# One batch of attention ahead of the products instead of two, in a fused attention and cosine feed-forward kernel

## The chip, the core and the metric

The kernel runs on one core of a Trainium2 chip. The metric is the time of one execution in microseconds on the device. Engines are called as in the profile: PE (TensorE), DVE (VectorE), ACT (ScalarE), POOL (GpSimd), and SP, whose queue issues most DMAs.

## The reference

```
# q, k, v: 8 batches, 8 heads, 576 positions, 64 dims
scores = (q @ k^T) / 8
heads 0-3 see keys with 0 <= i - j < 32; heads 4-7 keys with i >= j and i % 32 == j % 32
attn = softmax(masked scores);  o = attn @ v
x = o as 4608 tokens x 512
h = x @ w_in          # w_in 512 x 2048, double precision
g = h * cos(h)
out = g @ w_out       # w_out 2048 x 512, double precision
```

## The kernel before

**Attention by units.** A batch has 10 units: four "strided" ones (two pairs of heads, two halves of the residues) and six "local" ones (three stretches of 192 positions, two pairs of heads). A unit is a Python generator with three stages: scores and softmax; transposes of the probabilities; products with v. `schedule` lays these stages over numbered steps, `step(steps, n)` emits those of step n. KNOTS says how many units are begun by which step.

Units come in two kinds. With `plain` the softmax uses ACT's Exp, and the mask is written into the score bank by a matmul (L173). The others use two Silu passes and a square, since Silu and Sin share ACT's table, and add the mask on DVE. A unit loads q and k (`qk`) and v on SP's queue.

The results go to a DRAM tensor `xT`, 512 rows by 4608 tokens, by DMAs on ACT's queue (L260 and L320).

**The products by blocks and chunks.** A block is 384 tokens (12 blocks). A chunk is one of 16 pieces of 128 of the 2048 hidden columns, so there are 192 chunks. Both operands of each product are split into a rounded part and a rest (`hi`, `lo`), and three of the four products are taken. `hidden` (L345 and on) makes h with 12 matmuls of 384 columns, then g by ACT and DVE, then g's two parts; `outer` (L367) adds g times w_out into three accumulators, 9 matmuls of 512 columns. `outer` runs LAG = 3 chunks behind `hidden`. h has two banks.

`load_x(j)` brings block j's four pieces from `xT` into `x_raw`, casts them on DVE (L335) and subtracts on POOL (L336).

**The weights.** They arrive as doubles. `load_weight` (L111 to L130) loads 128 x 512 of them (512 KB) into one of two buffers `raw`, makes float32 words of them with three DVE passes (L116, L119, L125) and one ACT pass (L124), casts on ACT (L129) and subtracts on POOL (L130). Chunk f needs one such piece of w_in and one of w_out: 32 loads in all. From chunk AHEAD on, the conversion for chunk f is ordered behind the DVE reduction (L349) of chunk f - AHEAD of block 0.

**The order.** First the 20 plain units of batches 0 and 1, with `load_x(0)` and `load_x(1)` among them and some matmuls that only keep PE busy (L417). Then blocks 0 and 1 side by side: chunk f of block 0, then chunk f - 1 of block 1, so that each weight serves two chunks as it comes in. Then three chunks of block 2. Then one loop over the other chunks, with the 60 units of batches 2 to 7 among them.

The kernel is written in program order, but a scheduler fills each engine's queue: an instruction whose inputs and buffers are there may go ahead of earlier ones that wait. So a queue's order isn't the program's.

Of the kernel before, what the change touches and what calls it, by code (L numbers as in the profile page):

```python
# [36 lines left out]
NSU = -(-NG // SU)  # L37
MASKED = -8.0e9             # times the scale: the reference's -1e9
# [5 lines left out]
TB = 384                    # tokens of a block  # L44
# [8 lines left out]
LOADS = (12, 20)  # L53
# [15 lines left out]
def attention_cos_ffn(ctx, tc, qkl, vl, qkvs, w_in, w_out, eye, eye16, mask_l0, mask_l, mask_s, out):  # L69
# [7 lines left out]
    xp = ctx.enter_context(tc.tile_pool(name="xp", bufs=2))  # L77
# [10 lines left out]
    shift1, shift2 = (const.tile([P, 1], F32, name=n) for n in ("shift1", "shift2"))  # L88
    for t, value in ((shift1, -SHIFT), (shift2, -SHIFT - STEP)):
# [21 lines left out]
    def load_weight(cv, src, hi, lo, after):  # L111
        """src: 128 x 512 doubles; hi + lo: their float32."""
# [9 lines left out]
        # A double's upper word as a float32 has the exponent's upper eight bits; scaled, its exponent and mantissa  # L122
        # are the float32's, three bits too far right. What is below a float32's range becomes nothing.
# [279 lines left out]
    with ExitStack() as loading:  # L403
        cv = loading.enter_context(tc.tile_pool(name="cv", bufs=2))
        with ExitStack() as stack:
# [19 lines left out]
            for n in range(max(steps) + 1):  # L425
# [3 lines left out]
                if n == LOADS[0]:  # L429
                    x0 = load_x(0)  # L430
# [135 lines left out]
```

## Time and profile before

| | |
|---|---|
| three runs | 1002.9, 1004.25, 1005.04 us |
| median | 1004.25 us |
| span of the profiled execution, first to last instruction | 1000.8 us |
| median of the runs less that span | 3.45 us |
| PE busy | 984.5 us (98%) |
| ACT busy | 572.9 us (57%) |
| DVE busy | 464.6 us (46%) |
| POOL busy | 381.9 us (38%) |

The profiled execution has no time of its own beside its span; what lies around the span is taken as the 3.45 us. "Busy" is the union of an engine's instructions, and matmuls overlap one another, so the mean time of one matmul is longer than the time it adds; distances between starts tell what it adds. Rows of busy time by stretch read: stretch, its length, busy time of each engine with its number of instructions, granted clock of PE as a share of full speed, share of the DMA engines, GB/s. Rows of one line alone have only the engines that run that line.

### The profile page before, as it was taken

The page shows a single profiled execution, that of the slowest core. Times are in us where ns is not written, and L with a number is a line of the kernel's source. Part 1 is how long each engine was busy: PE and PEld are TensorE (multiplying, and loading weights), DVE is VectorE, ACT ScalarE, POOL GpSimd, SP SyncE. Part 2 cuts the span into 40 slices and gives each one's busy share as a digit, 9 for nine tenths or more (in the row PEclk, how much of TensorE's full clock was granted, in tenths as well). Part 3 has the DMA queues.
Part 4 walks back from the last instruction along what each step waited for, and adds up shares of the span by engine and source line. Part 5 has one row for each costly group of instructions (what it writes and reads, how often), then busy time and mean ns, then how long its engine had stood idle before and what let it go on. Part 6 is the DMA issues. An engine that isn't in the chain of part 4 may idle for free.

```text
span 1000.8 us, 17954 instructions
## 1 busy us (share of the span) xinstructions
PE 984.5 (98%) x6890; PEld 841.0 (84%) x6890; DVE 464.6 (46%) x1004; ACT 572.9 (57%) x1235; POOL 381.9 (38%) x418
## 2 busy tenths in 40 slices
PE   9989999999999999999999999999999999999998
PEld 5768877888888888888888888888888888889997
DVE  6866777645544444444344344434443444322222
ACT  3666666666665555555555555555655555544543
POOL 2654544624443443333333343323333333322222
PEclk9999999999999999999999999999999999999999
DMA  7963333122332223112212122211211221100000
GB/s 249 303 196 121 110 107 125 59 90 73 103 90 81 85 68 97 50 49 69 78 44 82 50 87 58 78 50 53 84 58 39 88 63 43 48 9 1 32 1 32
DMA packets 48230, 80.15 MB, mean 80 GB/s; under 512 B 5904, under 2 KB 33296, under 8 KB 48144
## 3 DMA queue, kind: packets, MB, share of 16 engines
q1 hardware_dynamic: 38208, 69.35, 22.3%
q10 hardware_dynamic: 9936, 9.65, 2.8%
q8 instruction: 54, 0.88, 0.4%
q14 instruction: 32, 0.26, 0.1%
HBM read 60.11 MB, written 18.87 MB: 79 GB/s over the span
## 4 chain that ended last, share of the span: by engine, by line
PE 84%; DMA 7%; DVE 5%; issue 2%; ACT 1%; POOL 0%; SPq 0%; ACTq 0%; DVEq 0%; POOLq 0%
PE h L345 37%; PE acc L367 35%; DMA raw<-in_w_out 4%; PE acc L238 3%; DVE raw L116 2%; PE acc L303 2%; PE acc L254 2%; PE acc L279 2%; PE acc L246 1%; DVE raw L119 1%; DVE raw L125 1%; DMA qk<-in_qkl 1%; PE acc L291 1%; PE acc L417 1%; DMA x_raw<-xT 1%
## 5 line engine op out<-in xcount | busy, mean ns | idle before, releaser
L360 POOL TENSOR_TENSOR g_lo<-r,g_hi 128x384 fp32r<-128x384 f32 x192 | 196.5, 1024 | 369.5 <-issue 246.6
L345 PE MATMUL h<-x_hi,wi_h 128*128 128x384 f32 x768 | 273.3, 356 | 7.8 <-DVE r L356 7.8
L345 PE MATMUL h<-x_lo,wi_h 128*128 128x384 f32 x768 | 259.1, 337 | 0.4 <-POOL x_lo L336 0.4
L345 PE MATMUL h<-x_hi,wi_l 128*128 128x384 f32 x768 | 259.4, 338 | 0.0
L349 DVE SCALAR_TENSOR_TENSOR r<-r,h 128x384 f32<-128x384 int32 x192 | 106.3, 554 | 276.1 <-ACT r L348 270.1
L367 PE MATMUL acc<-wo_l,g_hi 128*128 128x512 f32 x576 | 228.0, 396 | 0.0
L367 PE MATMUL acc<-wo_h,g_hi 128*128 128x512 f32 x576 | 227.7, 395 | 0.0
L367 PE MATMUL acc<-wo_h,g_lo 128*128 128x512 f32 x576 | 225.5, 396 | 0.0
L348 ACT ACTIVATE r<-h 128x384 int32<-128x384 f32 x192 | 93.9, 489 | 158.0 <-PE h L345 128.3
L345 PEld LDWEIGHTS h<-x_hi,wi_h 128*128 128x128 f32 x768 | 144.5, 188 | 27.5 <-DVE r L356 17.7
L356 DVE SCALAR_TENSOR_TENSOR r<-r,h 128x384 f32<-128x384 f32 x192 | 105.9, 552 | 107.3 <-ACT r L355 107.2
L345 PEld LDWEIGHTS h<-x_lo,wi_h 128*128 128x128 f32 x768 | 145.0, 189 | 3.0 <-POOL x_lo L336 0.7
L352 ACT ACTIVATE r<-r 128x384 f32<-128x384 f32 x192 | 100.2, 522 | 79.6 <-DVE r L349 79.5
L359 ACT CAST g_hi<-r 128x384 fp32r<-128x384 f32 x192 | 98.2, 511 | 82.8 <-DVE r L356 80.3
L345 PEld LDWEIGHTS h<-x_hi,wi_l 128*128 128x128 f32 x768 | 144.7, 188 | 0.2
L367 PEld LDWEIGHTS acc<-wo_h,g_lo 128*128 128x128 f32 x576 | 108.2, 188 | 24.9
L367 PEld LDWEIGHTS acc<-wo_h,g_hi 128*128 128x128 f32 x576 | 108.1, 188 | 18.1 <-ACT g_hi L359 0.3
L367 PEld LDWEIGHTS acc<-wo_l,g_hi 128*128 128x128 f32 x576 | 108.2, 188 | 17.9
L355 ACT ACTIVATE r<-r 128x384 f32<-128x384 f32 x192 | 100.4, 523 | 4.5
L336 POOL TENSOR_TENSOR x_lo<-x_raw,x_hi 128x384 fp32r<-128x384 f32 x48 | 50.6, 1057 | 107.7 <-DVE x_hi L335 106.8
L195 POOL TENSOR_TENSOR t_sb<-t_sb,mx 128x288 f32<-128x288 f32 (+1 forms) x60 | 41.5, 692 | 47.3 <-DVE mx L194 42.0
L214 POOL TENSOR_TENSOR e_sb<-e_sb,z 128x288 f32<-128x288 f32 x48 | 31.9, 666 | 40.0 <-DVE z L212 21.0
(66 smaller groups left out, 884.0 us busy)
## 6 DMA issues: line engine op xcount, KB each, us to landing
qk<-in_qkvs SPq DMA_DIRECT2D x32, 324.0 KB, 3.2
qk<-in_qkl SPq DMA_DIRECT2D x48, 208.0 KB, 2.5
x_raw<-xT SPq DMA_DIRECT2D x48, 192.0 KB, 2.4
out<-o SPq DMA_DIRECT2D x36, 256.0 KB, 2.1
raw<-in_w_in SPq DMA_DIRECT2D x16, 512.0 KB, 3.6
raw<-in_w_out SPq DMA_DIRECT2D x16, 512.0 KB, 3.6
v<-in_vl SPq DMA_DIRECT2D x48, 144.0 KB, 2.3
xT<-x_t ACTq DMA_DIRECT2D x16, 288.0 KB, 3.6
```

The costliest lines, as they stand in the source:

```text
L195: nc.gpsimd.tensor_tensor(out=t, in0=t, in1=mx[:, :n].unsqueeze(2).broadcast_to([P, n, w]), op=ALU.subtract)
L214: nc.gpsimd.tensor_tensor(out=pn, in0=e, in1=z[:, :n].unsqueeze(2).broadcast_to([P, n, w]), op=ALU.mult)
L336: nc.gpsimd.tensor_tensor(out=lo, in0=raw, in1=hi.bitcast(F32), op=ALU.subtract)
L345: nc.tensor.matmul(h, w[:, f, c], x[c], start=(i == 0), stop=(i == len(ops) - 1))
L348: nc.scalar.activation(out=k, in_=h, func=AF.Copy, scale=1.0 / (2.0 * math.pi))
L349: red = nc.vector.scalar_tensor_tensor(out=r, in0=k, scalar=-2.0 * math.pi, in1=h, op0=ALU.mult, op1=ALU.add)
L352: sin = nc.scalar.activation(out=r, in_=r, func=AF.Sin, scale=0.5)
L355: nc.scalar.activation(out=r, in_=r, func=AF.Square)
L356: nc.vector.scalar_tensor_tensor(out=r, in0=r, scalar=0.5, in1=h, op0=ALU.subtract, op1=ALU.mult)
L359: nc.scalar.copy(out=g_hi, in_=r)
L360: nc.gpsimd.tensor_tensor(out=g_lo, in0=r, in1=g_hi.bitcast(F32), op=ALU.subtract)
L367: nc.tensor.matmul(acc[t], g[:, ts], w[:, f], start=(f == 0 and i == 0), stop=(f == NFC - 1 and i == 2))
```

## The change

- Only the 10 units of batch 0 run as plain units ahead of the products. The 70 units of batches 1 to 7 are units of the Silu kind among the chunks.
- Blocks are no longer paired: one loop over all 192 chunks, with the weights' conversions among block 0's 16 chunks and units from its first step on. AHEAD is 3 instead of 2.
- Block 0's x doesn't go through `xT`: a unit's result is cast and subtracted straight from its SBUF tile (`keep`, `split_x`); the other columns are written as before.
- `load_x` loads into the tile of the low part instead of a buffer of its own.
- cos(h) is sin(r + pi/2) with the bias in a tile, where it was 1 - 2 sin(r/2)^2: the ACT pass for the square goes, DVE's last pass becomes a plain product, and the final copies lose their factor of -2.
- The units' tile `e_sb` has 2 buffers instead of 3, `v` 3 instead of 4, `o` 2 instead of 3 in the loop.

```
-AHEAD = 2
+AHEAD = 3
-KNOTS = ((LAG, 0), (9.5, 8), (25, 16), (121, 56), (131, 60))
-UNIT_LAG = 3
+KNOTS = ((0, 0), (9, 6), (52, 26), (100, 46), (148, 66), (164, 70))
+UNIT_LAG = 2
...
-            e = self.wk.tile([P, SU * GB], F32, name="e_sb", bufs=4 if self.plain else 3)
+            e = self.wk.tile([P, SU * GB], F32, name="e_sb", bufs=4 if self.plain else 2)
...
-            v = self.ld.tile([P, VS], F32, name="v", bufs=4)
+            v = self.ld.tile([P, VS], F32, name="v", bufs=3)
...
-            nc.scalar.dma_start(out=xT[:, 2 + p, at:at + LU * QB], in_=x_t)
+            self.keep(2 + p, b * S + u * LU * QB, x_t)
+
+        def keep(self, c, at, x_t):
+            n = x_t.shape[1]
+            first = min(max(TB - at, 0), n)
+            if first:
+                split_x(x_t[:, :first], x0[0][c][:, at:at + first], x0[1][c][:, at:at + first])
+            if first < n:
+                nc.scalar.dma_start(out=xT[:, c, at + first:at + n], in_=x_t[:, first:])
...
+    def split_x(x, hi, lo):
+        nc.vector.tensor_copy(out=hi, in_=x)
+        nc.gpsimd.tensor_tensor(out=lo, in0=x, in1=hi.bitcast(F32), op=ALU.subtract)
...
-            raw = xp.tile([P, TB], F32, name="x_raw")
+            raw = lo.bitcast(F32)
...
-        nc.scalar.activation(out=k, in_=h, func=AF.Copy, scale=1.0 / (2.0 * math.pi))
+        nc.scalar.activation(out=k, in_=h, func=AF.Copy, scale=1.0 / (2.0 * math.pi), bias=0.25)
...
-        sin = nc.scalar.activation(out=r, in_=r, func=AF.Sin, scale=0.5)
+        sin = nc.scalar.activation(out=r, in_=r, func=AF.Sin, bias=quarter)
...
-        nc.scalar.activation(out=r, in_=r, func=AF.Square)
-        nc.vector.scalar_tensor_tensor(out=r, in0=r, scalar=0.5, in1=h, op0=ALU.subtract, op1=ALU.mult)
+        nc.vector.tensor_tensor(out=r, in0=r, in1=h, op=ALU.mult)
...
+        units = att.units(0)
+        steps = schedule(units, ((0, 0), (len(units), len(units))), 2)
...
+        steps = schedule([unit for b in range(1, B) for unit in att.units(b)], KNOTS, UNIT_LAG)
+        nxt = x0
+        for n in range(NTB * NFC):
+            j, f = n // NFC, n % NFC
             if f == 0:
                 cur, acc = nxt, accumulators(ps_o)
+            if j == 0:
+                need_weights(cv, f)
             step(steps, n)
             if f == LOAD_AT and j + 1 < NTB:
                 nxt = load_x(j + 1)
             chunk(j, f, cur, acc)
+            if j == 0:
+                need_weights(cv, min(f + AHEAD, NFC - 1))
```

More of the change, by code (lines that the diff above doesn't have):

```diff
@@ L326, in units, with x_operands @@
             ]
[L328 to L333 removed]
+    def split_x(x, hi, lo):
+        nc.vector.tensor_copy(out=hi, in_=x)
+        nc.gpsimd.tensor_tensor(out=lo, in0=x, in1=hi.bitcast(F32), op=ALU.subtract)
+    def x_operands():
+        return tuple([xs.tile([P, TB], F32R, name=name) for _ in range(NKC)] for name in ("x_hi", "x_lo"))
+    def load_x(j):
+        his, los = x_operands()
+        for c, (hi, lo) in enumerate(zip(his, los)):
+            raw = lo.bitcast(F32)
             nc.sync.dma_start(out=raw, in_=xT[:, c, j * TB:(j + 1) * TB])
[L335 to L338 removed]
+            split_x(raw, hi, lo)
         return his, los
@@ L401, in step @@
             next(unit, None)
-    with ExitStack() as loading:
-        cv = loading.enter_context(tc.tile_pool(name="cv", bufs=2))
-        with ExitStack() as stack:
-            ps = stack.enter_context(tc.tile_pool(name="ps", bufs=1, space=bass.MemoryType.PSUM, reuse_waits="tile"))
-            att = Attention(
-                stack, True, ((ps_h, "h"), (ps_h, "h"), (ps, "acc0")), ((ps_o, "acc0"), (ps_o, "acc1")),
-                ((ps_o, "acc2"), (ps, "acc3")), ld_bufs=3,
-            )
-            steps = schedule(att.units(0) + att.units(1), ((0, 0), (20, 20)), 2)
-            spare = ps.tile([P, 512], F32, name="acc2")
-            def keep_busy(n, after):
-                for _ in range(n):
-                    mm = nc.tensor.matmul(
-                        spare[:64], warm, warm.unsqueeze(1).broadcast_to([P, 8, 64]), start=True, stop=True
-                    )
-                    if after is not None:
-                        order(mm, after, "in its place")
-                    after = mm
-            keep_busy(BUSY[0], None)
-            for n in range(max(steps) + 1):
-                step(steps, n)
-                if n + 1 < len(BUSY):
-                    keep_busy(BUSY[n + 1], att.scored)
-                if n == LOADS[0]:
-                    x0 = load_x(0)
-                if n == LOADS[1]:
-                    x1 = load_x(1)
-        gp = ctx.enter_context(tc.tile_pool(name="gp", bufs=LAG + 1, side="right", reuse_waits="tile"))
-        with ExitStack() as stack:
-            op = stack.enter_context(tc.tile_pool(name="op", bufs=2, reuse_waits="tile"))
-            ps_o1 = stack.enter_context(
-                tc.tile_pool(name="ps_o1", bufs=1, space=bass.MemoryType.PSUM, reuse_waits="tile")
-            )
-            acc0, acc1 = accumulators(ps_o), accumulators(ps_o1)
-            for f in range(NFC + 1):
-                if f < NFC:
-                    need_weights(cv, f)
-                    chunk(0, f, x0, acc0)
-                    need_weights(cv, min(f + AHEAD, NFC - 1))
-                if f >= 1:
-                    chunk(1, f - 1, x1, acc1)
-            cur, acc = load_x(2), accumulators(ps_o)
-            for f in range(LAG):
-                chunk(2, f, cur, acc)
@@ L454, in attention_cos_ffn, with keep_busy @@
-    with ExitStack() as stack:
-        op = stack.enter_context(tc.tile_pool(name="op", bufs=3, reuse_waits="tile"))
+    x0 = x_operands()
+    cv = ctx.enter_context(tc.tile_pool(name="cv", bufs=2))
+    with ExitStack() as stack:
+        ps = stack.enter_context(tc.tile_pool(name="ps", bufs=1, space=bass.MemoryType.PSUM, reuse_waits="tile"))
+        att = Attention(
+            stack, True, ((ps_h, "h"), (ps_h, "h"), (ps, "acc0")), ((ps_o, "acc0"), (ps_o, "acc1")),
+            ((ps_o, "acc2"), (ps, "acc3")), ld_bufs=3,
+        )
+        units = att.units(0)
+        steps = schedule(units, ((0, 0), (len(units), len(units))), 2)
+        spare = ps.tile([P, 512], F32, name="acc2")
+        def keep_busy(n, after):
+            for _ in range(n):
+                mm = nc.tensor.matmul(
+                    spare[:64], warm, warm.unsqueeze(1).broadcast_to([P, 8, 64]), start=True, stop=True
+                )
+                if after is not None:
+                    order(mm, after, "in its place")
+                after = mm
+        keep_busy(BUSY[0], None)
+        for n in range(max(steps) + 1):
+            step(steps, n)
+            if n + 1 < len(BUSY):
+                keep_busy(BUSY[n + 1], att.scored)
@@ L456, in attention_cos_ffn @@
+    gp = ctx.enter_context(tc.tile_pool(name="gp", bufs=LAG + 1, side="right", reuse_waits="tile"))
+    op = ctx.enter_context(tc.tile_pool(name="op", bufs=2, reuse_waits="tile"))
+    with ExitStack() as stack:
         ps = stack.enter_context(tc.tile_pool(name="ps", bufs=1, space=bass.MemoryType.PSUM, reuse_waits="tile"))
         att = Attention(stack, False, *(((ps, f"acc{i}"),) for i in range(3)), ld_bufs=2)
-        steps = schedule([unit for b in range(2, B) for unit in att.units(b)], KNOTS, UNIT_LAG)
```

25 lines of the change are left out of this document (6 added, 19 removed).

## The prediction

> **What bounds the kernel now.** I read the page's totals first, then the busy time by stage, then the chain that ended last, and then the rows of the weight conversion.
>
> ```profile
> span 1000.8 us, 17954 instructions
> PE 984.5 (98%) x6890; PEld 841.0 (84%) x6890; DVE 464.6 (46%) x1004; ACT 572.9 (57%) x1235; POOL 381.9 (38%) x418
> ...
> L355 ACT ACTIVATE r<-r 128x384 f32<-128x384 f32 x192 | 100.4, 523 | 4.5
> ```
> ```profile
> 0.00:48.60 48.60, 45.81 (x674) 30.75 (x675) 36.03 (x110) 24.11 (x59) 21.54 (x31) 1.00 0.86 279
> 48.60:75.00 26.40, 21.21 (x162) 17.90 (x160) 16.19 (x33) 17.68 (x40) 14.27 (x14) 0.95 0.62 194
> 98.00:187.00 89.00, 85.36 (x403) 70.91 (x402) 65.51 (x97) 60.02 (x115) 44.63 (x38) 1.00 0.34 113
> 200.00:873.00 673.00, 673.00 (x4871) 579.24 (x4870) 292.30 (x672) 389.31 (x863) 250.06 (x288) 1.00 0.23 69
> ```
> The columns are stretch, length, then busy time of PE, PEld, DVE, ACT and POOL. From 200 to 873 us PE is busy 673.00 of 673.00: there the time is the sum of PE's work, and other engines have room (ACT 389). All that can be lost or won lies before 200 us, where attention and weights come first. So I price PE's work, and then ask how long PE waits early on.
>
> ```profile
> 916.39 2.11 PE h L345 x12
> ...
> 987.91 2.11 PE h L345 x12
> 990.02 5.84 PE acc L367 x25
> ```
> ```profile
> 200.00:1000.80 800.80, 376.23 (x1920) 330.66 (x1920) 1.00 0.20 60
> ```
> ```profile
> 200.00:1000.80 800.80, 367.31 (x1462) 271.67 (x1460) 1.00 0.20 60
> ```
> The first fence is the chain: 17 chunks lie between its first two rows, (987.91 - 916.39) / 17 = 4.207 us a chunk, half of it the 12 matmuls of `hidden`, half the 9 of `outer`. The work ends at 995.86; 4.94 us of copy, store and end follow. The other two, busy time of one line's instructions, count L345 and L367 after 200 us: 1920/12 = 160 hidden halves and 1462/9 = 162.4 outer halves, 322.4 x 2.1035 = 678.2 us. Of 795.86 us, 117.7 are left for 60 units of attention: **1.95 us of PE a unit**.
>
> Now the weights. The chain runs through them between 98 and 187 us.
>
> ```profile
> 144.27 3.51 DMA raw<-in_w_out
> ...
> 153.56 3.63 DMA raw<-in_w_out
> ```
> ```profile
> L116 DVE TENSOR_SCALAR raw<-raw x32: 385/859/1547, 12.2 to 185.4; 128x512 int32<-128x512 int32 x32
> L119 DVE SCALAR_TENSOR_TENSOR raw<-raw x32: 678/694/1684, 13.4 to 186.6; 128x512 int32<-128x512 int32 x32
> L124 ACT ACTIVATE raw<-raw x32: 658/666/712, 14.1 to 187.4; 128x512 f32<-128x512 f32 x32
> L125 DVE SCALAR_TENSOR_TENSOR raw<-raw x32: 649/693/1250, 15.3 to 188.1; 128x512 int32<-128x512 int32 x32
> ...
> L129 ACT CAST wi_h<-raw x16: 656/667/680, 15.9 to 184.2; 128x512 fp32r<-128x512 f32 x16
> L130 POOL TENSOR_TENSOR wi_l<-raw,wi_h x16: 1307/1316/1787, 16.7 to 185.0; 128x512 fp32r<-128x512 f32 x16
> ...
> DMA to landing us min/median/max: 3.4/3.6/6.7
> ```
> Loads of w_out start 153.56 - 144.27 = 9.29 us apart. `raw` has two buffers, one for w_in's chunk and one for w_out's, and a buffer takes its next load only when L130 is through with it. So a buffer's own loop is the DMA, three DVE, two ACT steps and one POOL step; by medians, with L116 at its shortest, 3.6 + 0.385 + 0.694 + 0.666 + 0.693 + 0.667 + 1.316 = 8.0 us. The missing 1.3 us are mostly L116, whose median is 0.859; two rows of the timeline say why:
>
> ```profile
> 143.68 0.85 DVE L116 TENSOR_SCALAR raw<-raw 128x512 int32<-128x512 int32 x1
> ```
> ```profile
> 142.93 1.31 POOL L130 TENSOR_TENSOR wo_l<-raw,wo_h 128x512 fp32r<-128x512 f32 x1
> ```
> It starts while L130 runs on POOL and ends 0.29 us after POOL's end (144.24). Sixteen pairs at 9.29 us are 149 us, whatever PE does. Before, two chunks share each pair, 2 x 4.207 = 8.4 us of PE per 9.29, so PE hardly waits: 85.36 of 89.00.
>
> **The change, part by part.**
>
> *Ten units leave the front.* Before, chunk 0 waits for x0, which goes through HBM (rows of the timeline: start, length, engine and line):
>
> ```profile
> 36.80 0.32 ACT L258 COPY x_l<-acc 128x192 f32<-128x192 f32 x1
> ```
> ```profile
> 43.42 0.90 SPq L334 DMA_DIRECT2D x_raw<-xT  x2
> ```
> ```profile
> 48.60 0.42 PE L345 MATMUL h<-x_hi,wi_h 128*128 128x384 f32 x1
> ```
> The last copy that block 0 needs ends at 37.1, its loads are issued at 43.4, and the product starts at 48.6. On chip it is one cast and one subtraction, about 1.5 us, so 38.6 without anything else; and as batch 1's units no longer stand among batch 0's on DVE I take 32 (ends: 28 and 40). The cast waits for ACT's copy, and on DVE softmaxes and conversions stand behind it; six casts in place of eight, so I count nothing for that. The other end matters little, since the weights come later still. The writes of block 0's part of xT on ACT's queue and its four loads on SP's go. The mask matmuls of ten units go too, in time that was idle.
>
> *The same ten units come back in the loop*, as Silu units: 10 x 1.95 = 19.5 us of PE, certain. In total PE's work after the front is 192 x 4.207 + 70 x 1.95 = 944.2 us, with the tail 949.2. From 32 us on that would be 981 us if PE never waited.
>
> *Block 0 takes the weights alone.* One chunk and few units stand against each pair. First the start: with AHEAD = 3, f = 2 waits for no chunk.
>
> ```profile
> 28.91 1.32 POOL L130 TENSOR_TENSOR wi_l<-raw,wi_h 128x512 fp32r<-128x512 f32 x1 [2.26 <-ACT wi_h L129]
> ```
> ```profile
> 33.28 0.38 SPq L114 DMA_DIRECT2D raw<-in_w_in  x1
> ```
> ```profile
> 53.98 1.31 DVE L116 TENSOR_SCALAR raw<-raw 128x512 int32<-128x512 int32 x2
> ```
> Before, f = 1's buffer is free at 30.2, the load of f = 2 is issued at 33.3 (SP stood behind x's and v's loads), and its conversion starts at 53.98, after chunk 0's reduction. After, load at 30, landing at 33.6, L116 at 34: the stream is 20 us earlier. From there 13 periods lead to f = 15, and the rest of the loop, 9.29 - 3.6 = 5.7 us, to its split weights. The period's ends are 8.0 and about 10.5 (both L116 at its longest, 2 x (1.547 - 0.859) = 1.4 more); I take 9.29, the row nearest to it, as unit work replaces the second chunk's. So 34 + 13 x 9.29 + 5.7 = 160.5, and 162.6 with the last hidden half.
>
> *What PE can do meanwhile.* Sixteen hidden and 13 outer halves (61.0 us), and units. By the order of steps alone 6 + (16 - 9) x 20/43 = 9.3 units are begun at step 16. But the queues are filled ahead: weights already convert at 12.2 us here, though the program has them after all attention. So I let units run until DVE is full (two groups of the page, then busy times of three stretches, the second for the casts of x alone):
>
> ```profile
> L349 DVE SCALAR_TENSOR_TENSOR r<-r,h 128x384 f32<-128x384 int32 x192 | 106.3, 554 | 276.1 <-ACT r L348 270.1
> L356 DVE SCALAR_TENSOR_TENSOR r<-r,h 128x384 f32<-128x384 f32 x192 | 105.9, 552 | 107.3 <-ACT r L355 107.2
> ```
> ```profile
> 116.56:125.84 9.28, 8.90 (x43) 7.40 (x43) 6.92 (x11) 6.28 (x13) 4.70 (x4) 1.00 0.33 113
> ```
> ```profile
> 200.00:873.00 673.00, 13.72 (x35) 1.00 0.23 69
> ```
> ```profile
> 15.00:45.00 30.00, 28.85 (x470) 20.55 (x468) 27.96 (x85) 18.33 (x48) 17.54 (x21) 1.00 0.87 282
> ```
> A chunk costs DVE 1.106 us. A pair of weights with two chunks keeps it 6.92, with one 5.81. A unit costs at most (292.30 - 13.72 for x's casts - 132 x 1.106) / 60 = 2.2 us (132 chunks: 160 less the (990.0 - 873) / 4.207 = 28 after 873). In the front DVE reached 27.96 of 30, 93%; of 9.29 that is 8.65, so (8.65 - 5.81) / 2.2 = 1.29 units a period, 17.6 over 13.6 periods, and one at the start: 18.6 units (ends: 9.3 and 22).
>
> *Cosine as sine.* ACT loses one pass a chunk, 523 ns (L355), and its Sin takes a bias tile; DVE's last pass stays one pass over the same two operands. At 389 of 673 us ACT isn't what PE waits for, so 0; in block 0 it takes 0.5 us from ACT's 6.28 a period, where DVE is fuller. The shorter path from h to g ends a last chunk sooner, hidden behind the 5.84 us of outer halves at the end.
>
> *Fewer buffers* (e_sb 3 to 2, v 4 to 3, o 3 to 2), load_x into x_lo, the knots: between 0 and some 5 us if a unit came late in the loop; 0 taken, as PE was never idle there, and the units (after block 0 some 51 to 176 chunks) come no closer than before (60 to 157). Should one be late, its transposes wait on PE's queue and the chunk's matmuls stand behind them.
>
> **Sum.** 162.6 + 176 x 2.1035 + 179 x 2.1035 + (70 - 18.6) x 1.95 + 4.94 = 162.6 + 746.7 + 100.2 + 4.9 = 1014.4 us of span. The three runs have a median of 1004.25, 3.45 over the profiled span, so **1017.9, say 1017 us, 1.3% slower**. The front wins some 16 us; PE then waits about 33 us in block 0 for weights.
>
> **Rivals.**
>
> *A, faster: the pairs come at 8.0 us and DVE runs full.* Speaking for it: the stream is no longer tied to two chunks in ACT's and DVE's order. Against: L116 is met by POOL whenever POOL works, and units add two POOL passes. 34 + 13 x 8.0 + 4.4 + 2.1 = 144.5; DVE free per period 8.0 - 5.81 + 0.95 = 3.1 us, 1.4 units, 20 in all; 144.5 + 746.7 + 97.5 + 4.9 = 993.6 of span, 997. It decides from a period of some 8.6 with 1.3 units. (The Trainium skill, GPSIMD Engine Reference, specifications, says that POOL's SBUF interfaces are shared with VectorE and contended by DVE instructions in a two-port mode or with two SBUF inputs. By that rule the added POOL passes keep L116 slow and A falls; the trace agrees for L116, 0.85 beside POOL against 0.385, but L119, with two SBUF inputs, stays at 0.69.) If weights never came late it would be 981 + 3.5 = 985.
>
> *B, slower still: units don't run ahead.* 9.3 units by the end of block 0: 9.3 x 1.95 = 18 us more, 1036; with a DVE so much freer the period may be 9.0, 1032. For it: units share one bank per stage, so the second waits for the first.
>
> *C, PE drops to half clock in block 0.*
>
> ```profile
> 72.28 0.59 PE L345 MATMUL h<-x_hi,wi_h 128*128 128x384 f32 x1 [2.31 <-DVE r L356]
> ```
> ```profile
> 72.28 3.91 PE h L345 x12
> ```
> ```profile
> 73.00:74.00 1.00, 1.00 (x5) 1.00 (x5) 0.69 (x2) 0.96 (x2) 1.00 (x2) 0.50 0.11 37
> ```
> After 2.31 us without work the granted clock is 0.50 and the 12 matmuls take 3.91 instead of 2.11: 1.8 us. Once in each of 13 periods is 23 us; PE is idle 9.29 - 4.21 - 2.52 = 2.6 us a period, so most is swallowed; half of it on the path gives 1029. (The Trainium skill, TensorE: Matmul & The Clock Gate, "HAM oscillation", puts the limit at PE-idle gaps over about 3.4 us. By it gaps of 2.6 us would cost nothing and the sum stays 1017; the row above shows a drop after 2.31, so I keep C.)
>
> **How the numbers follow.** Three runs spread 1002.9 to 1005.04, so 0.2% (1002.2 to 1006.3) is what I call no change. Forecast (1006 to 1025): 0.45. A: 0.25. B and C (1025 to 1036): 0.20. Between forecast and A, within 0.2%: 0.10. So faster 0.25, same 0.10, slower 0.65. The range 996 to 1031 leaves about a tenth on each side; the forecast's own is 1006 to 1025.
>
> **What would show it.** First product near 32 us instead of 48.6. L116's first f = 2 near 34. Loads of w_in 9 us apart to about 150, and PE in 40 to 160 us busy about 70 to 75%, with DVE near 93%. Between 15 and 22 units begun at 160. After that PE full, 4.207 a chunk and 1.95 a unit. Wrong would be: pairs under 8.6 us, PE over 85% busy in block 0, or PE waiting in the main loop.

## The result, and the profile after

The changed kernel takes 1048.0 us against 1004.6 us before: ratio 1.044, 95% interval 1.042 to 1.046. The direction was forecast, the size (1017) not: 31 us more than the forecast, and 17 above the upper end of the range. The profiled execution has a span of 1045.0 us, 30.6 above the predicted 1014.4.

Line numbers move by three: the weights' steps are now L111 (load), L113, L116 (DVE), L121 (ACT), L122 (DVE), L126 (ACT cast), L127 (POOL); before they were L114, L116, L119, L124, L125, L129, L130. The `hidden` products are L352, the copy of h that follows a chunk's last one is L356.

Page of the kernel after, totals and slices:

```profile
span 1045.0 us, 17835 instructions
PE 1004.2 (96%) x6879; PEld 853.0 (82%) x6879; DVE 489.5 (47%) x1017; ACT 516.8 (49%) x1063; POOL 401.0 (38%) x430
...
PE   9787888899999999999999999999999999999997
DVE  6789898732323434434433443433434433422221
PEclk9898888899999999999999999999999999999999
```

Busy time by stretch, first of the kernel after, then of the kernel before (columns as in the prediction):

```profile
35.00:195.00 160.00, 128.65 (x1115) 101.40 (x1116) 140.75 (x255) 104.01 (x220) 100.84 (x95) 0.86 0.57 181
200.00:880.00 680.00, 680.00 (x4532) 585.88 (x4532) 271.85 (x595) 329.62 (x679) 234.92 (x265) 1.00 0.19 57
```
```profile
35.00:195.00 160.00, 150.35 (x944) 126.18 (x941) 112.80 (x197) 105.19 (x214) 84.78 (x78) 0.99 0.43 139
```

Apart from the last slice, which holds the end, the weak slices of the PE row, its eights and sevens, lie before 210 us. Between 200 and 880 us PE is busy 680.00 of 680.00, so nearly all of the loss is made before. Between 35 and 195 us PE has 31 us without work, and the granted clock of what it does is 0.86; DVE is busy for 141 us instead of 113.

Timeline of the kernel after, single rows (start, length, engine and line): first product, first passes for w_in of chunks f = 2, 4 and 15, and the copy of h of chunk 15 of block 0:

```profile
27.00 0.43 PE L352 MATMUL h<-x_hi,wi_h 128*128 128x384 f32 x1
...
32.91 0.90 DVE L113 TENSOR_SCALAR raw<-raw 128x512 int32<-128x512 int32 x1 [1.07 <-DMA raw<-in_w_in]
...
54.42 1.31 DVE L113 TENSOR_SCALAR raw<-raw 128x512 int32<-128x512 int32 x1 [0.71 <-DMA raw<-in_w_in]
...
181.90 0.42 DVE L113 TENSOR_SCALAR raw<-raw 128x512 int32<-128x512 int32 x1
...
193.74 0.47 ACT L356 ACTIVATE r<-h 128x384 int32<-128x384 f32 x1
```

The front came as forecast (f = 2 at 32.9, forecast 34). But pairs of weights then came every (181.90 - 32.91) / 13 = **11.46 us**, not 9.29, and block 0's last hidden half ended at 193.7, not 162.6. These 31.1 us are the miss: 13 x (11.46 - 9.29) = 28.2 from the pace and 4.0 from the last pair's way to the end of its products (11.8 us, forecast 7.8), less 1.1 for the earlier start. Four more units than forecast had begun by then (23, forecast 18.6), worth -8.6 us; the stretch from there to the end took 8.0 us more than its terms. That these two cancel, so that the sum agrees with the 30.6, is chance. Of the 8.0, 1.5 lie at the very end: the last copy of results now waits 2.1 us for a transfer to free one of two buffers `o`, and 6.4 us follow PE's last product where 4.94 were taken. The rest wasn't split further; three of the 23 units weren't through at 193.7.

DVE's groups between 60 and 180 us of the kernel after (busy time, mean ns of one, idle time before):

```profile
L116 DVE SCALAR_TENSOR_TENSOR raw<-raw 128x512 int32<-128x512 int32 x21 | 22.7, 1083 | 0.2
L122 DVE SCALAR_TENSOR_TENSOR raw<-raw 128x512 int32<-128x512 int32 x20 | 17.4, 869 | 1.6 <-ACT raw L121 1.6
L202 DVE SCALAR_TENSOR_TENSOR e_sb<-t_sb,e_sb 128x288 f32<-128x288 f32 (+1 forms) x20 | 15.8, 792 | 2.5 <-ACT t_sb L201 2.5
L113 DVE TENSOR_SCALAR raw<-raw 128x512 int32<-128x512 int32 x21 | 14.7, 698 | 3.1 <-DMA raw<-in_w_out 1.4 <-DMA raw<-in_w_in 1.3 <-issue 0.3
L208 DVE TENSOR_SCALAR z<-z 128x3 f32<-128x3 f32 (+1 forms) x19 | 10.1, 530 | 0.2
```

The reader should see two things. The idle column is nearly empty: DVE goes from one instruction to the next. And the durations aren't those of the work: L208 adds a constant to 3 or 6 numbers a row and takes 530 ns on average. All L208, and all L116, of the run (min/median/max in ns):

```profile
L208 DVE TENSOR_SCALAR z<-z x80: 152/170/1271, 9.2 to 904.4; 128x3 f32<-128x3 f32 x48, 128x6 f32<-128x6 f32 x32
```
```profile
L116 DVE SCALAR_TENSOR_TENSOR raw<-raw x32: 644/1012/1805, 10.8 to 188.2; 128x512 int32<-128x512 int32 x32
```

Two pairs of rows of the timeline after, POOL and DVE side by side:

```profile
99.80 1.29 POOL L127 TENSOR_TENSOR wo_l<-raw,wo_h 128x512 fp32r<-128x512 f32 x1 [1.31 <-ACT wo_h L126]
...
100.04 1.08 DVE L208 TENSOR_SCALAR z<-z 128x3 f32<-128x3 f32 x1
...
113.36 1.55 POOL L127 TENSOR_TENSOR wo_l<-raw,wo_h 128x512 fp32r<-128x512 f32 x1
...
113.79 1.67 DVE L116 SCALAR_TENSOR_TENSOR raw<-raw 128x512 int32<-128x512 int32 x1
```

POOL ends at 101.09 and L208 at 101.12; POOL ends at 114.91 and L116 at 115.46. The same holds throughout: of 27 L116 between 35 and 195 us, 14 are over 1.3 times their shortest, and each of those ends 0.55 us after a POOL instruction's end; of 21 L208, 15 are, each ending 0.02 to 0.03 us after one. L113 (0.28 to 0.29 after), L122 (0.55) and L202 (0.31 to 0.36) do the same. DVE's passes that read PSUM (L190, L357, L363), its reductions and its reciprocals are never long there. Of all instructions of the other six kinds (L113, L116, L122, L202, L208 and the cast L334) in this stretch, 89 begin while POOL is at work, and 72 of them are long; 45 begin while it isn't, and none is. So such a DVE instruction that begins beside a POOL instruction mostly stands until that one is through, and the wait counts as busy. (The Trainium skill, SBUF — State Buffer, "Who interferes with whom", calls DVE's and GpSimd's shared port pair "an exclusive lock": the one that comes second is blocked until the first is through. The constant distance from POOL's end agrees.) For each long instruction in which a POOL instruction ends I take its duration less the shortest of its line and shape. These add up to 40.7 of DVE's 140.75 us; in the kernel before, to 20.7 of 112.80. I call this sum **DVE's standing**.

### The profile page after: what moved, and what is told of

It is laid out like the page before. It is cut to its first block, busy times and chain, and to the rows that moved or that the text cites. A ratio compares the mean times of both kernels' runs of the same rounds, so it can differ in the third digit from the quotient of the medians.

```text
span 1045.0 us, 17835 instructions
## 1 busy us (share of the span) xinstructions
PE 1004.2 (96%) x6879; PEld 853.0 (82%) x6879; DVE 489.5 (47%) x1017; ACT 516.8 (49%) x1063; POOL 401.0 (38%) x430
## 4 chain that ended last, share of the span: by engine, by line
PE 82%; DVE 6%; issue 1%; DMA 1%; ACT 1%; POOL 1%; DVEq 0%; ACTq 0%; POOLq 0%
PE h L352 38%; PE acc L374 36%; PE acc L235 2%; PE acc L308 2%; PE acc L251 2%; PE acc L284 1%; PE acc L243 1%; DVE z L208 1%; PE acc L296 1%; DVE raw L122 1%; DVE e_sb L202 1%; DVE raw L113 1%; DVE raw L116 1%; DVE t_sb L190 1%; DVE z L207 0%
## 5 line engine op out<-in xcount | busy, mean ns | idle before, releaser
L352 PE MATMUL h<-x_hi,wi_h 128*128 128x384 f32 x768 | 271.0, 353 | 12.4 <-ACT wi_h L126 4.7
L352 PE MATMUL h<-x_hi,wi_l 128*128 128x384 f32 x768 | 263.4, 343 | 0.4 <-POOL wi_l L127 0.4
L357 DVE SCALAR_TENSOR_TENSOR r<-r,h 128x384 f32<-128x384 int32 x192 | 106.0, 552 | 335.8 <-ACT r L356 312.7
L352 PE MATMUL h<-x_lo,wi_h 128*128 128x384 f32 x768 | 263.1, 343 | 0.0
L356 ACT ACTIVATE r<-h 128x384 int32<-128x384 f32 x192 | 94.1, 490 | 163.4 <-PE h L352 159.1
L352 PEld LDWEIGHTS h<-x_hi,wi_h 128*128 128x128 f32 x768 | 146.4, 191 | 26.1 <-ACT wi_h L126 5.7
L360 ACT ACTIVATE r<-r,quarter 128x384 f32<-128x384 f32 x192 | 118.2, 616 | 93.1 <-DVE r L357 92.0
L352 PEld LDWEIGHTS h<-x_lo,wi_h 128*128 128x128 f32 x768 | 146.7, 191 | 5.4
L363 DVE TENSOR_TENSOR r<-r,h 128x384 f32<-128x384 f32 x192 | 106.0, 552 | 94.5 <-ACT r L360 93.9
L352 PEld LDWEIGHTS h<-x_hi,wi_l 128*128 128x128 f32 x768 | 146.2, 190 | 2.4 <-POOL wi_l L127 0.9
L335 POOL TENSOR_TENSOR x_lo<-x_lo,x_hi 128x384 fp32r<-128x384 f32 x44 | 46.3, 1056 | 46.1 <-DVE x_hi L334 41.4
L192 POOL TENSOR_TENSOR t_sb<-t_sb,mx 128x288 f32<-128x288 f32 (+1 forms) x70 | 51.3, 733 | 29.2 <-DVE mx L191 27.9
L200 ACT ACTIVATE e_sb<-t_sb,shift 128x288 f32<-128x288 f32 (+1 forms) x70 | 38.3, 547 | 40.6 <-POOL t_sb L192 38.6
L202 DVE SCALAR_TENSOR_TENSOR e_sb<-t_sb,e_sb 128x288 f32<-128x288 f32 (+1 forms) x70 | 42.1, 601 | 16.3 <-ACT t_sb L201 16.3
```

The source lines that it names most:

```text
L192: nc.gpsimd.tensor_tensor(out=t, in0=t, in1=mx[:, :n].unsqueeze(2).broadcast_to([P, n, w]), op=ALU.subtract)
L200: nc.scalar.activation(out=e, in_=t, func=AF.Silu, bias=shift1, scale=0.0625)
L202: nc.vector.scalar_tensor_tensor(out=e, in0=t, scalar=-math.exp(STEP), in1=e, op0=ALU.mult, op1=ALU.add)
L335: nc.gpsimd.tensor_tensor(out=lo, in0=x, in1=hi.bitcast(F32), op=ALU.subtract)
L352: nc.tensor.matmul(h, w[:, f, c], x[c], start=(i == 0), stop=(i == len(ops) - 1))
L356: nc.scalar.activation(out=k, in_=h, func=AF.Copy, scale=1.0 / (2.0 * math.pi), bias=0.25)
```

## The experiments

Theories. **Q**: the units' steps stand among the conversion's passes in DVE's full queue. **P**: POOL's passes slow DVE's. **R**: a raw buffer's round (load, passes, next load), with two buffers, is the pace. **S**: DVE and ACT stand at a chunk's range reduction while its products wait. (D in some expectations is Q.) "Pace" below is from first pass to first pass for w_in, f = 4 to f = 15, over 11 (the expectations mostly give it from f = 2).

| kernel | pace | chunk 15's h | units begun | DVE busy 35-195 | standing | time | ratio (interval) |
|---|---|---|---|---|---|---|---|
| after | 11.59 | 193.7 | 23 | 140.8 | 40.7 | 1048.0 | 1.044 (1.042-1.046) |
| units_tied | 10.92 | 186.0 | 10 | 112.5 | 26.7 | 1059.2 | 1.055 (1.053-1.057) |
| units_late | 10.40 | 180.4 | 7 | 113.1 | 26.1 | 1060.8 | 1.057 (1.054-1.061) |
| sub_on_dve | 11.29 | 196.0 | 23 | 137.7 | 20.1 | 1044.5 | 1.041 (1.039-1.042) |
| two_passes | 10.79 | 184.2 | 23 | 121.2 | 30.3 | 1039.5 | 1.035 (1.031-1.039) |
| three_raw | 10.02 | 174.3 | 17 | 137.0 | 40.7 | 1040.7 | 1.036 (1.034-1.038) |
| tied_three_raw | 9.27 | 163.6 | 10 | 131.8 | 40.2 | 1038.4 | 1.033 (1.031-1.035) |
| late_three_raw | 8.78 | 157.7 | 7 | 127.4 | 37.3 | 1039.6 | 1.035 (1.033-1.038) |
| three_raw_two | 7.94 | 142.8 | 10 | 111.6 | 28.8 | 1020.9 | 1.016 (1.014-1.019) |
| three_raw_two_dense | 8.25 | 147.9 | 13 | 123.0 | 35.4 | 1021.0 | 1.016 (1.014-1.019) |

Parts and cures in the kernel before (no units beside blocks 0 and 1 there, so a pair's passes share the queues with two chunks). Each "before" was measured again beside its run, at 1004.0 to 1004.8 us; the ratios go by these:

| kernel | pace | time | ratio (interval) |
|---|---|---|---|
| before | 9.40 | 1004.6 | |
| before_x0 | 9.83 | 1009.8 | 1.005 (1.003-1.006) |
| before_sine | 9.55 | 1003.0 | 0.999 (0.997-1.001) |
| before_ahead3 | 10.17 | 1013.5 | 1.009 (1.007-1.011) |
| before_sine_ahead3 | 9.79 | 1003.8 | 0.999 (0.998-1.001) |
| before_raw3 | 9.14 | 1006.7 | 1.002 (1.001-1.003) |
| before_two | 9.04 | 1008.1 | 1.002 (1.000-1.004) |
| before_raw3_two | 8.49 | 998.8 | 0.994 (0.992-0.996) |
| before_raw3_sine | 9.16 | 1002.7 | 0.998 (0.996-1.000) |
| before_raw3_two_sine | 8.37 | 990.9 | 0.987 (0.985-0.990) |

### Units held back

`units_tied`: a unit's mask addition stands behind the latest range reduction, so units begin at their steps.

```
-                nc.vector.tensor_tensor(out=t, in0=s, in1=mask, op=ALU.add)
+                add = nc.vector.tensor_tensor(out=t, in0=s, in1=mask, op=ALU.add)
+                if reduced:
+                    order(add, reduced[-1], "units no earlier than their step")
```


> The changed kernel with each unit's first DVE step ordered behind the last reduction of h, so that no unit runs ahead of its step in block 0. Theory Q (units that run ahead stand between the weights' steps on DVE and stretch the 11.46 us period of the changed kernel): about 9 units instead of 22 by the end of block 0, a period near 9.5, that end at 170 instead of 194, and 13 units x 2 us given back later, so 1045 to 1052 in all: no gain. Theory P (POOL's work holds DVE's steps): fewer POOL passes too, a period near 9.8. Theory R (the two raw buffers alone set the period): it stays at 11.4 and the time rises by 26 us to 1074.

`units_late`: the same, and none before chunk 9.

```
-KNOTS = ((0, 0), (9, 6), (52, 26), (100, 46), (148, 66), (164, 70))
+KNOTS = ((9, 0), (9.9, 6), (16, 6.01), (56, 26), (100, 46), (148, 66), (164, 70))
```


> As units_tied, with no unit before step 9 of block 0, six of them there, and the rest from step 16 on. Q: between chunks 3 and 9 nothing but one chunk stands beside a pair of weights, and the period is 8.0 to 8.5; then it rises. In all about 1045 to 1055, as every unit that block 0 doesn't take costs 2 us later. P: L127 and g_lo still meet DVE's steps, so 9.0 to 9.5. R: 11.4.

Both are slower than the change as it is: a unit that isn't done in block 0 is done later, where PE is full. So the units' running ahead, which I had priced as a gain, is one here; with a third buffer (below) it is none. In block 0 of `units_tied`:

```profile
35.00:195.00 160.00, 117.66 (x769) 94.67 (x765) 112.52 (x192) 87.74 (x170) 86.95 (x79) 0.81 0.45 147
```

DVE is busy for 70% and the pace is 10.9 all the same. So Q alone, a full DVE, falls as the cause: with 10 units it expected a period near 9.5. R alone expected 11.4 and 1074 us, and falls as well. `units_late` shows the floor. Its timeline, one buffer from pass to pass, and f = 3 and 8, between which no unit runs:

```profile
45.23 0.43 DVE L113 TENSOR_SCALAR raw<-raw 128x512 int32<-128x512 int32 x1 [1.20 <-DMA raw<-in_w_in]
...
63.94 0.70 DVE L113 TENSOR_SCALAR raw<-raw 128x512 int32<-128x512 int32 x1 [1.74 <-DMA raw<-in_w_in]
...
64.67 0.69 DVE L116 SCALAR_TENSOR_TENSOR raw<-raw 128x512 int32<-128x512 int32 x1
65.45 0.66 ACT L121 ACTIVATE raw<-raw 128x512 f32<-128x512 f32 x1 [2.17 <-DVE raw L116]
66.14 0.69 DVE L122 SCALAR_TENSOR_TENSOR raw<-raw 128x512 int32<-128x512 int32 x1 [0.31 <-ACT raw L121]
66.86 0.65 ACT L126 CAST wi_h<-raw 128x512 fp32r<-128x512 f32 x1 [0.26 <-DVE raw L122]
...
67.59 1.30 POOL L127 TENSOR_TENSOR wi_l<-raw,wi_h 128x512 fp32r<-128x512 f32 x1 [3.24 <-ACT wi_h L126]
...
68.92 0.33 SPq L111 DMA_DIRECT2D raw<-in_w_in  x1
...
72.88 1.52 DVE L113 TENSOR_SCALAR raw<-raw 128x512 int32<-128x512 int32 x1 [0.82 <-DMA raw<-in_w_in]
...
92.01 1.47 DVE L113 TENSOR_SCALAR raw<-raw 128x512 int32<-128x512 int32 x1 [0.87 <-DMA raw<-in_w_in]
```

Each step begins as the last one ends, and the next load goes out 0.03 us after L127: 8.94 us, and (92.01 - 45.23) / 5 = 9.36 on average. This is R's round with no unit in its way. The predicted 9.29 was thus about the round without units; whatever a unit puts between two of its steps comes on top.

### POOL's pass on DVE, and one DVE pass less

```
-        nc.gpsimd.tensor_tensor(out=lo, in0=w, in1=hi.bitcast(F32), op=ALU.subtract)
+        nc.vector.tensor_tensor(out=lo, in0=w, in1=hi.bitcast(F32), op=ALU.subtract)
```


> The changed kernel with the weights' subtraction (L127) on DVE instead of POOL. P: POOL loses 2.8 us a period, and DVE's L116 and L122 fall from 1.03 and 0.84 us to 0.70; the buffer's loop loses 1.31 and gains 0.6; period 10 us, time 1025 to 1032. Q: DVE, full already, gets 1.2 us more a period, period 12 or more, time 1052 to 1058.

The pace stays at 11.3, and the 1044.5 us lie between P's numbers and Q's. This looks like P refuted, but isn't. L116 of this kernel:

```profile
L116 DVE SCALAR_TENSOR_TENSOR raw<-raw x32: 651/692/1486, 11.3 to 187.3; 128x512 int32<-128x512 int32 x32
```

Its median fell from 1012 to 692 ns and DVE's standing from 40.7 to 20.1 us, but the 28 moved passes in the stretch, at 0.66 us or more each, put 21.9 us back on the same queue. The run moved the cost and doesn't decide on P.

```
-        first = nc.vector.tensor_scalar(out=low, in0=low, scalar1=29, ..., op0=ALU.logical_shift_right)
+        first = nc.vector.tensor_scalar(out=low, in0=top, scalar1=-0x80000000, ..., op0=ALU.bitwise_and)
...
-        nc.vector.scalar_tensor_tensor(
-            out=low, in0=top, scalar=-0x80000000, in1=low, op0=ALU.bitwise_and, op1=ALU.bitwise_or
-        )
```


> The changed kernel with two DVE passes per weight instead of three: the sign is cut from the upper word and the lower word's three bits are left out, so each weight lacks its last three bits. Q and P both: DVE loses 2 x 0.74 us a period and the loop one step; period near 9.8, time 1022 to 1030 if DVE sets the period. If PE's half clock in block 0 (granted 0.86 between 35 and 195 us) sets it (theory C), the time stays at 1045 to 1048.

DVE has 20 us less to do and the pace falls by 0.8 only: something else binds at once. The expected pace was 9.8 and the time 1022 to 1030; both were missed.

### The third raw buffer

```
-    cv = ctx.enter_context(tc.tile_pool(name="cv", bufs=2))
+    cv = ctx.enter_context(tc.tile_pool(name="cv", bufs=3))
-    op = ctx.enter_context(tc.tile_pool(name="op", bufs=2, reuse_waits="tile"))
+    op = ctx.enter_context(tc.tile_pool(name="op", bufs=1, reuse_waits="tile"))
-                self.x_t[key] = self.wk.tile([P, S], F32, name="x_t")
+                self.x_t[key] = self.wk.tile([P, S], F32, name="x_t", bufs=2 if self.plain else 1)
```


> The changed kernel with a third raw buffer for the weights' conversion (the output tiles and the attention's x_t go from two buffers to one to make room). Theory R, a raw buffer's round (transfer, five passes over three engines, next transfer) is what a pair of weights takes: with three buffers a round of 11.5 us has a buffer free half as often again, the period of a pair falls from 11.46 towards the DVE work of 10.9 us that it holds now, or below it if fewer units get in between; last hidden half of block 0 at 165-180 instead of 194, time 1020-1035. Theory D, DVE's queue is full in block 0 (its idle time from 60 to 180 us is under 10 us), so the period is the DVE work between two pairs, whatever the number of buffers: period 10.8-11.3, last hidden half 186-192, time 1041-1048. The single output buffer may cost up to 2 us a block where a copy waits for the transfer before it, so up to 10 us on top if it shows.

With the units as they are, the buffer alone wins 7 us: block 0 ends within R's range, the time lies just under D's. These 7 us are net of 2.7 that the single output buffer adds behind PE's last product. The same with the units tied (`tied_three_raw`) and with them late (`late_three_raw`):

> The same third buffer in the kernel whose units are held to their steps, where DVE is busy for only 70% of block 0 and the period is 11.0 all the same. Theory R: the period falls to 8-9.5 us (DVE work a period 7.7 us), last hidden half of block 0 at 145-165 instead of 186, time 1020-1040. Theory S, the queues couple conversion and products (DVE and ACT stand at a chunk's range reduction while its products wait for weights): the third buffer lies idle behind the same waits, period 10.3-11, time 1052-1060. Theory D has nothing to say on this one, as DVE has 30% to spare.

> The kernel with its units held to late steps (six at chunk 9, the others from chunk 16 on) and a third raw buffer. With two buffers its pairs without units beside them came every 9.4 us. If that was the round of a raw buffer, three buffers bring the pairs without units to 6.5-7.5 us (DVE work without units: 6.4 us a pair in the profile of the changed kernel), chunk 15 at 140-150 and the time to 1035-1045, limited by PE's own idle time as no units fill it. If the conversion's serial passes on ACT, POOL and DVE or the chunk behind it set 9.4, the pace stays at 9-9.4 and the time at 1055-1061.

Here the buffer wins 21 us in each. In `late_three_raw`, from f = 5 to f = 9, where no unit runs:

```profile
64.52 0.43 DVE L113 TENSOR_SCALAR raw<-raw 128x512 int32<-128x512 int32 x1 [1.50 <-DMA raw<-in_w_in]
...
92.44 0.87 DVE L113 TENSOR_SCALAR raw<-raw 128x512 int32<-128x512 int32 x1 [0.44 <-DMA raw<-in_w_in]
```
```profile
64.00:92.40 28.40, 20.33 (x80) 15.12 (x78) 25.79 (x34) 16.58 (x31) 15.60 (x12) 0.88 0.42 132
```

(92.44 - 64.52) / 4 = 6.98 us a pair against 9.36 with two buffers: R holds where no unit stands in DVE's queue. But DVE is now busy 25.79 of 28.40 without a single unit. S falls as the main cause: the tied kernel's pace went below its 10.3. So two limits lie close together, the round at 9.4 and DVE at 7.0 and up, about 2.9 us more for each unit (the means of its six passes in the window 60 to 180: L202, L208 above, and L191, L207, L190, L209 at 0.46, 0.45, 0.47, 0.17).

`three_raw_two` takes both away: the third buffer and the pass.

> The changed kernel with the third raw buffer and one DVE pass less in the conversion of the weights (the weights lose their last three bits). If the ring's latency and DVE's load bind in turn (either alone moved the period by 1.1 and 0.5 us: 11.46 to 10.35 and 11.0), both together give more than their sum: period 8.8-9.5, last hidden half of block 0 at 155-165, time 1025-1032. If they only add: period 9.9, last hidden half near 167, time 1032-1037. If something else holds the period near 10 (the chunk's own chain from products to the next conversion), the time stays at 1038-1041.

```profile
45.30 0.42 DVE L113 TENSOR_SCALAR raw<-raw 128x512 int32<-128x512 int32 x1
...
132.62 0.49 DVE L113 TENSOR_SCALAR raw<-raw 128x512 int32<-128x512 int32 x1 [0.66 <-DMA raw<-in_w_in]
```
```profile
35.00:195.00 160.00, 142.83 (x1116) 116.64 (x1113) 111.56 (x207) 104.55 (x214) 102.95 (x97) 0.99 0.48 152
```

(132.62 - 45.30) / 11 = 7.94 us. The buffer alone won 7.3 us of time, the pass alone 8.5, both 27.1. PE's idle time between 35 and 195 falls from 31 to 17 us and its clock rises to 0.99. That is more than the sum, and more than I expected of it; by block 0's end, too, it is 19.4, 9.5 and 51.0 us. It shows that the round and DVE's queue bind in turn. One thing besides differs: `three_raw_two` begins only 10 units in block 0, where the changed kernel begins 23. With 10 in each, `units_tied`, `tied_three_raw` and `three_raw_two` have 10.92, 9.27 and 7.94: the buffer takes 1.65 off the pace and the pass, behind it, 1.33 (the first two kernels hold their units by an order, the third doesn't). More units in block 0 (`three_raw_two_dense`) bring nothing:

```
-KNOTS = ((0, 0), (9, 6), (52, 26), (100, 46), (148, 66), (164, 70))
+KNOTS = ((0, 0), (16, 16), (52, 30), (100, 46), (148, 66), (164, 70))
```


> The changed kernel with a third raw buffer, one DVE pass less (the weights lose their last three bits) and one unit a chunk in block 0 (16 by chunk 16; 10 had begun by chunk 15 with the plan as it is). PE was busy for 142.8 of the 160 us between 35 and 195, of which block 0 had all the idle time. If the idle time is filled by units (1.95-2.1 us of PE each), six more are worth up to 12 us less what they cost DVE: 1010-1018. If they slow the conversion as in the changed kernel (a unit's 2.9 us of DVE work, which is at 70% here), block 0 ends 10-20 us later and the time is 1020-1030.

Three units more, block 0 5.1 us later: 1021.0 against 1020.9. At this load a unit costs the weights about what it saves PE.

### Parts of the change alone, in the kernel before

`before_x0`: `keep` and `split_x` as in the change, `load_x(0)` gone.

> The kernel before with one part of the change alone: block 0's x split where the attention leaves it, without the round trip through DRAM. There the first product waited for that round trip. If the first product then starts about 10 us earlier (37-40 us instead of 48.6) and the conversion of the weights follows, as the changed kernel's head suggests, time 994-1000; if the conversion of f=1 and 2 is late by then (the ring's rate, not the head, sets when the products are done), the start is earlier and the end is not: 1001-1005.

The first product starts at 48.9 us, before at 48.6: the round trip through HBM was not what it waited for. The last piece of x is split by 42.1 us, and PE goes on with matmuls of the 20 units in front until the first product. The part alone loses 5 us, more than either case expected; why isn't shown.

`before_ahead3`: `AHEAD = 3`. `before_sine`: the cosine lines of the change. `before_sine_ahead3`: both.

> The kernel before with another small part alone: the weights' conversion may run three chunks ahead of the products instead of two. In the kernel before the third pair lay in its buffers from about 39 us and its first pass started at 54.0, behind the first range reduction. Theory R: the conversion starts 10 us earlier and the chunks of blocks 0 and 1 follow: first passes of f=2 near 40, chunk pairs 5-8 us earlier, time 996-1000. Rival: the conversion takes DVE and ACT from the last attention units before the products, and the first product comes later by what the conversion gains, as with the third buffer in the kernel before (first pass of f=2 there at 58.8, first range reduction 2.2 us later): 1002-1006.

> The kernel before with one part of the change alone: the cosine as a shifted sine (a square pass less on ACT; the sine itself is 0.09 us longer by the changed kernel's profile). ACT bounds neither block 0 nor the later blocks, where PE is full: 1002.5-1006, no difference. Rival: the chain from the hidden products to the outer ones is half a microsecond shorter, and blocks 0 and 1, where PE waits for 5 to 6% of the time, gain: 998-1002.

> Both small parts in the kernel before. If each is worth what its first theory says, 993-998; if neither is, 1002-1006. More than their sum would mean that one opens what the other closed.

The sine alone is no difference, as forecast. AHEAD = 3 alone loses 9 us, which neither case had: the conversion starts at 41 instead of 54 us, but the first product comes at 53.4 instead of 48.6, and the pace is 10.17 instead of 9.40. Its timeline, POOL and DVE:

```profile
110.28 1.49 POOL L130 TENSOR_TENSOR wi_l<-raw,wi_h 128x512 fp32r<-128x512 f32 x1
```
```profile
110.64 1.68 DVE L119 SCALAR_TENSOR_TENSOR raw<-raw 128x512 int32<-128x512 int32 x1
```

L119, too, now meets POOL's L130 (ending at 111.77) and ends 0.55 us after it. Between 35 and 195 us 12 of 28 L119 are long, before 2 of 28; DVE's standing is 27.8 us instead of 20.7. That this is the cause isn't shown: in `before_sine_ahead3` 15 of 28 L119 are long and the standing is 27.4, and yet nothing is lost (first product at 50.7, pace 9.79). Why AHEAD = 3 costs 9 us alone and nothing beside the sine stays open. Whether AHEAD = 2 would help the changed kernel wasn't tried.

### The same cures in the kernel before

The edits shown above, of the third buffer's only the line of `cv`: the third buffer (`before_raw3`), the pass less (`before_two`), both, and the third buffer with the sine, without and with the pass less.

> The kernel before with a third raw buffer and nothing else. Its pairs come every 9.29 us against 8.41 us of products for the two blocks that share them. Theory R: period 8.4-8.6, PE idle of block 0 and 1 (10 us of the 160 between 35 and 195) mostly gone, time 993-999. Theory S or D: the period stays, 1002-1005.

> The kernel before with one DVE pass less in the conversion (the weights lose their last three bits), two raw buffers as before. If a raw buffer's round and DVE's passes bind in turn, as in the changed kernel, the pass alone moves the period little: 8.9-9.2 us, time 999-1004. If DVE's passes alone set it, the period is 8.3-8.5 with two buffers as well and the time 996-1000, as with three.

> The kernel before with a third raw buffer and one DVE pass less in the conversion (the weights lose their last three bits). If the products of the two blocks set the 9.2-9.3 us of its pairs (the third buffer alone did not move it), the period stays at 8.9-9.3 and the time at 1000-1007. If DVE's passes in the queue set it, the period falls to 8.4-8.6 and the time to 990-998.

> The kernel before with a third raw buffer and the cosine as a shifted sine; the weights keep all their bits. The sine takes a pass of ACT from each chunk, in whose queue two passes of the conversion stand. If the conversion's passes on ACT and DVE wait behind the chunk's passes, a shorter chunk lets them through: period 8.6-9.0, time 995-1001. If the DVE pass is what counts, the period stays at 9.2 and the time at 1001-1006, as the third buffer and the sine alone had it (1006.7 and 1003.0).

> The same with the cosine as a shifted sine, so that ACT has a pass less between the hidden and the outer products too (the weights lose their last three bits). If the chain from the hidden to the outer products is what is left of PE's waits in blocks 0 and 1 (PE's waits there were for the last DVE pass of that chain, 7.8 us in all), it is 3-8 us faster than the kernel before, 996-1001; if not, 1002-1006.

Timeline and stretch of `before_raw3_two` (f = 4 and 15), and the same rows of the kernel before:

```profile
74.70 1.10 DVE L116 TENSOR_SCALAR raw<-raw 128x512 int32<-128x512 int32 x2
...
168.08 0.76 DVE L116 TENSOR_SCALAR raw<-raw 128x512 int32<-128x512 int32 x2
```
```profile
35.00:195.00 160.00, 154.26 (x1030) 136.02 (x1030) 83.42 (x179) 107.73 (x223) 87.61 (x81) 0.99 0.44 140
```
```profile
77.66 0.43 DVE L116 TENSOR_SCALAR raw<-raw 128x512 int32<-128x512 int32 x1 [0.29 <-DMA raw<-in_w_in]
...
181.10 0.85 DVE L116 TENSOR_SCALAR raw<-raw 128x512 int32<-128x512 int32 x1
```

Before: 103.44 / 11 = 9.40; cured: 93.38 / 11 = 8.49, near the 2 x 4.207 = 8.41 of the products, so there PE sets it: the 9.29 was the conversion's own, as the second theory had it, though it needed both edits to show. The buffer alone or the pass alone leaves 9.0 to 9.1 and no gain in time, less than the 7 and 9 us in the changed kernel. With the sine on top, worth more than expected here (7.9 us), PE is busy 156.66 of these 160 us:

```profile
35.00:195.00 160.00, 156.66 (x1019) 138.87 (x1020) 86.90 (x179) 98.72 (x196) 90.80 (x82) 0.99 0.45 143
```

`before_raw3_two_sine` is the fastest of all, 990.9 us, 1.3% under the kernel before, with three bits of the weights left out. With all bits (`before_raw3_sine`) 0.998 (0.996 to 1.000) is no gain clear of the noise.

## Why the prediction was wrong

**Right.** The frame: nearly all is decided before 200 us; after that PE is full and the time is a sum. f = 2's first pass at 32.9 (34). DVE near 93% in block 0 (140.75 of 160 is 88%; 111.70 of 120 between 60 and 180 is 93%). Units run ahead (23, forecast 18.6 with the end at 22). The sine without effect as an edit of its own (beside AHEAD = 3 it is worth 9.7 us, in the cured kernel 7.9; why isn't shown). The sign. Not right was "0 taken" for fewer buffers: the end costs 1.5 us more with two buffers `o`.

**The step that failed** is "The period's ends are 8.0 and about 10.5; I take 9.29, the row nearest to it, as unit work replaces the second chunk's." It measured 11.46. Three things were wrong in it.

First, 9.29 was read as a pace that includes DVE's other work. `units_late` shows 9.36 with no unit beside the pairs: it is the bare round of two buffers, beside one chunk.

Second, I gave the weights their pace and the units the rest of DVE, "until DVE is full". A queue does not share so: a unit's passes stand in front of the next conversion pass, and with two buffers that delay goes straight into the round. Between f = 3 and f = 15 22 units entered in 12 periods, 1.8 each where I had 1.29.

Third, a unit cost 2.9 us of DVE and not 2.2, which came from the stretch after 200 us, and the passes were longer. Conversion 2 x (1.08 + 0.87 + 0.70) = 5.30, a chunk 1.08, 1.8 units 5.2: 11.6 us, about the whole 11.46. Records overlap a little at their ends, so DVE's union is less, 111.70 / 120 x 11.46 = 10.7. These durations contain standing behind POOL, and the upper end, "both L116 at its longest", let only one pass per weight stand (and 9.29 + 1.4 is 10.7, not 10.5). Per period the standing is 40.7 x 11.46 / 160 = 2.9 us after and 20.7 x 9.40 / 160 = 1.2 before: the difference, 1.7, compares with a missing 2.2, but it counts some of the same microseconds as the added units do. That POOL is the cause of the standing is shown by the distances from its ends; that the pace would fall by as much without it is worked out and not shown, as the one run that moved POOL's pass put it on DVE.

In the prediction's place stands: a round of some 9.4 us with two buffers, into which the passes of 1.8 units a pair, at 2.9 us each, are put on a DVE that is 93% busy, so that a pair takes 11.46. The runs with the third buffer and the pass less show both limits; how much of it is POOL's stays open.

**The rivals.** A had the wrong side of the trace. Its evidence against the rule of shared SBUF interfaces, "L119, with two SBUF inputs, stays at 0.69", held only because L119 seldom came while POOL was at work: its row has a longest of 1684 ns, and 2 of 28 were long. In the changed kernel that pass has a median of 1.01 us, and with AHEAD = 3 alone in the kernel before it is 1.68 beside L130. B had the sign of the units right, but its price was too high: 13 units fewer in `units_tied` cost 25.4 us at 1.95 each, less 7.7 won in block 0, some 18 in sum; measured 11. C's clock is there: 0.86 between 35 and 195, and in the timeline of the kernel after, a gap and the matmuls behind it:

```profile
46.32 0.69 PE L352 MATMUL h<-x_hi,wi_h 128*128 128x384 f32 x1 [3.47 <-DVE r L363]
...
48.09 0.52 PE L352 MATMUL h<-x_hi,wi_l 128*128 128x384 f32 x1
48.41 0.52 PE L352 MATMUL h<-x_hi,wi_h 128*128 128x384 f32 x1
48.73 0.52 PE L352 MATMUL h<-x_lo,wi_h 128*128 128x384 f32 x1
```

Starts are 0.32 us apart, at full clock 2.1035 / 12 = 0.175. In `three_raw_two` the clock is 0.99 and the time 27 us less, but how much of it is the clock's wasn't measured by itself. That the clock sets the pace of 11.46 is unlikely: a period needs 4.2 + 1.8 x 1.95 = 7.7 us of PE at full clock, some 9.0 at 0.86, and `late_three_raw` came to 6.98 at 0.88. (The Trainium skill, TensorE: Matmul & The Clock Gate, "HAM oscillation", speaks of gaps over about 3.4 us. Here the matmuls at 37.3 us follow a gap of 2.32 us, and from 39.35 us on the starts are 0.32 us apart; so here, too, a shorter gap was followed by half clock.)

**The part on x.** "On chip it is one cast and one subtraction ... so 38.6 without anything else" was wrong as a part: alone it moved the first product by +0.3 us. In the change the first product came at 27.0, since ten units left the front, but it came in pieces as x arrived, and the chunk was through at 42.3 against 52.6 before.

## What to carry to other kernels

A step that goes round over several engines and few buffers has a bare round, and everything else in the same queues adds to it; read the round where nothing else runs, then add what the change puts in between, and don't hand out an engine's free share. When a buffer alone and a pass alone each win little, try both together before dropping either: here 7 and 9 us alone, 27 together. And before summing DVE durations, look at their spread: where the shortest and the median differ, the rest is another engine's time, and it moves with the phase.

## What the hardware showed that I had not expected

A DVE instruction with two SBUF inputs, or a tensor-scalar or copy within SBUF, that begins while a POOL instruction is at work mostly ends a fixed time after POOL's end (72 of 89 in block 0 of the changed kernel): 0.55 us for 128 x 512 with two inputs, 0.28 for one, 0.03 for three numbers a row. So the smallest instruction can be the dearest one: 80 additions of a constant have a median of 0.17 us and a longest of 1.27.

How often an instruction meets POOL moves with small shifts: with the conversion one chunk earlier and nothing else changed, 12 of 28 L119 stood instead of 2. That kernel lost 9 us, but the same standing beside the sine lost none, so it isn't shown that the one caused the other.
